# Attention output normalised by VectorE's 32x32 transposes, one power in the mixer's double layer norm, grouped tail tiles

## Chip, cores and metric

One core of one Trainium2 chip. The metric is the device time of one execution in microseconds (us), as the median of several executions. The profile of a kernel is one execution; its span is 1 to 2 us shorter than the device time of the same run.

Engines in the profile: PE is TensorE, PEld its weight loads, DVE is VectorE, ACT is ScalarE, POOL is GpSimd, SP is SyncE. In lines of the profile, `L1178` is a line of the kernel, `out<-in` are the program's names, `xN` is a count.

## The reference

Two identical layers, each of attention and a mixer, over `x` of 1 x 2048 x 448, 16 heads of 28:

```python
def _layernorm(x, eps=1e-5):
    m = jnp.mean(x, axis=-1, keepdims=True); v = jnp.var(x, axis=-1, keepdims=True)
    return (x - m) / jnp.sqrt(v + eps)

def _A_ref(x, wqkv, wo):                       # attention
    q, k, v = split_heads(x @ wqkv)            # ... cut
    p = softmax(einsum("bhqd,bhkd->bhqk", q, k) * 28 ** -0.5)
    return merge_heads(einsum("bhqk,bhkd->bhqd", p, v)) @ wo

def _B_ref(x, w1, w2, w3, w4):                 # mixer
    h  = gelu(_layernorm(x) @ w1)              # then four channel groups shifted by -1, +1, -2, +2 rows
    x1 = x + shifted(h) @ w2                   # ... cut
    return x1 + gelu(_layernorm(x1) @ w3) @ w4

x = x + _A_ref(_layernorm(x), ...); x = x + _B_ref(_layernorm(x), ...)    # twice
```

The mixer is called on `_layernorm(x)` and normalises that input again: a layer norm of a layer norm.

## The kernel before

A scheduler in Python plans all instructions of all engines from a list of tasks, by a plan of latest starts. `MOVES`, a list of (time, seed) pairs found by a search, perturbs the plan. The instruction order on each engine is fixed when the kernel is built, so the order is part of the kernel. When TensorE would idle in the plan, the scheduler puts filler matmuls on `ones_bf` there. They compute nothing; they keep its clock up (shown for the setup: between 12 and 14 us it was 0.50 before and 1.00 in e1, which adds 22 of them; 1.00 after and 0.50 in e2, which takes 17 away).

The normalisation of the attention output, 36 times per execution. `u_sb` holds heads x 32 rows on the partitions; row 28 of each 32 is the softmax sum. TensorE moves the sums across partitions, VectorE takes reciprocals and splits them into two bf16 parts, and TensorE spreads them back:

```python
def t_norm(si):                                          # before; waits and buffer handling cut
    if first: dve: u_sb = copy(ps[UBK])                  # 128 x W out of the PV bank
    else:     dve: u_sb = uin * fct + ps[UBK]
    # ... if not last: spill u_sb to DRAM, return
    dve: ub = cast_bf16(u_sb)
    for q4 in range(nq): pe: ps[b][:, 4*q4:4*q4+4] = ub[:, 128*q4:128*q4+128].T @ e28b      # sums
    dve: rs = reciprocal(ps[b]);  dve: rh[0:m] = bf16(rs);  dve: rh[16:16+m] = rs - rh[0:m]
    pe:  ps[b][0:32, 0:128] = rh.T @ ident
    dve: rT = copy(ps[b])
    for q4 in range(nq): pe: ps[b][:, 128*q4:...] = selq[:, 128*q4:...].T @ rT              # spread
    dve: otn[:, g, 0:W] = u_sb * ps[b]
```

The mixer's double layer norm has two powers in a chain, on GpSimd, with small VectorE steps between:

```python
def t_mixA(L, tiles, direct):                            # before; cut
    dve:  VAR = var + EPS
    pool: R1  = VAR ** -0.5
    dve:  T1 = R1 * R1;  dve: T1 = T1 * var;  dve: T1 = T1 + EPS
    pool: R12 = T1 ** -0.5
    dve:  R12 = R12 * R1
    for t in tiles: dve: xn = (x_res[t] - mean) * R12
    transposes(xn, xt)                                   # a DMA transpose
```

ScalarE evaluates the softmax exponentials out of PSUM, 2 or 3 banks of 512 columns at a time. Scores are written ahead into five banks, so TensorE and ScalarE overlap as long as the scores come in time (they are busy for 96% and 95% of the span).

## Time and profile before

Median of 4 runs 1104.1 us (1103.57 to 1109.55); span of the profiled run 1103.0 us.

| stretch of ScalarE's timeline | us |
|---|---|
| start to the first exponential | 31.7 |
| first to the end of the last exponential | 1026.6, of it 14.8 waiting |
| end of the last exponential to the end | 44.7 |

The page of the kernel before: busy time and share by engine, then TensorE's clock in 40 slices (tenths of full speed), the chain of work that ended last, and the costliest groups.

```profile
PE 1054.4 (96%) x9277; PEld 416.9 (38%) x9277; DVE 616.1 (56%) x1546; ACT 1049.8 (95%) x960; POOL 57.1 (5%) x82
...
PEclk7999999999999999999999999999999999999999
...
ACT 71%; PE 23%; DVE 4%; DMA 1%; issue 0%; SPq 0%; POOL 0%; ACTq 0%; DVEq 0%
...
L1178 ACT ACTIVATE PT<-ps 128x1536 bf16<-128x1536 f32 (+1 forms) x821 | 937.3, 1257 | 14.3 <-PE ps L1152 7.9
...
L1532 PE MATMUL ps<-ones_bf 128*128 128x256 bf16 x1153 | 173.0, 277 | 3.1 <-DVE ones_f L677 1.1
```

ScalarE is the bound: the chain is 71% ScalarE, and 937 of 1103 us are exponentials. TensorE's 96% contains 173 us of fillers. The only slice with a low clock is the first; a second half clock, of 3.4 us at 384 us, is too short to show in a slice.

The setup in windows of the kernel before: the window, its length, busy time of each engine with instruction counts, then the granted clock, DMA share and GB/s.

```profile
8.00:10.00 2.00, 0.82 (x10) 0.64 (x7) 0.00 (x0) 1.01 (x3) 2.00 (x4) 1.00 0.44 95
10.00:12.00 2.00, 0.38 (x6) 0.33 (x7) 0.93 (x2) 2.00 (x4) 1.79 (x3) 0.94 1.19 307
12.00:14.00 2.00, 1.75 (x13) 0.85 (x11) 1.33 (x8) 2.00 (x5) 0.60 (x1) 0.50 1.55 392
...
22.00:24.00 2.00, 2.00 (x6) 0.69 (x5) 1.50 (x5) 0.54 (x1) 0.87 (x1) 0.50 0.00 0
24.00:26.00 2.00, 2.00 (x8) 0.80 (x7) 1.03 (x3) 0.95 (x3) 0.00 (x0) 0.65 0.00 0
```

TensorE idles for 2.8 us (8.8 to 11.6), and its clock is halved from 11.8 until about 25.4 us, though from 12 to 26 us it is busy for 84% to 100% of each window of 2 us but one (20 to 22 us: 63%).

The tail in the chain of waits of the kernel before: start, us, what. It runs from the last normalisation to the first matmul on the transposed tile.

```profile
1065.55 0.15 DVE mst L1323
...
1067.57 0.54 POOL mst L1328
...
1068.13 0.17 DVE mst L1329
...
1068.33 0.53 DVE xn L1331
...
1068.89 2.30 DMA xT<-xn
```

### The profile page before, as it was taken

How to read it: one execution, taken by the hardware profiler on the slowest of the kernel's cores; microseconds unless marked ns; L12 is line 12 of the kernel's file. 1: busy time of each engine (PE TensorE's matmuls, PEld its weight loads, DVE VectorE, ACT ScalarE, POOL GpSimd, SP SyncE). 2: the span in 40 equal slices, each digit the busy share in tenths (PEclk: the TensorE clock that was granted, in tenths of full speed). 3: DMA queues.
4: the chain of work that ended last, by engine and by line, in shares of the span. 5: the costliest groups of instructions: out<-in, count | busy, mean ns of one | idle time of the engine just before them, and what ended most of it. 6: DMA issues, size and time to landing. Idle time of an engine off the chain costs nothing.

```text
span 1103.0 us, 21497 instructions
## 1 busy us (share of the span) xinstructions
PE 1054.4 (96%) x9277; PEld 416.9 (38%) x9277; DVE 616.1 (56%) x1546; ACT 1049.8 (95%) x960; POOL 57.1 (5%) x82
## 2 busy tenths in 40 slices
PE   8999999999999999999999999999999999999998
PEld 4333333343333333333333433343333333444465
DVE  5975247422654356743787354525886446486464
ACT  6999999999999999999799999999999999999954
POOL 3100000000000000000001000000010000010000
PEclk7999999999999999999999999999999999999999
DMA  7222071000000010000121101221201011100001
GB/s 194 58 86 59 20 190 21 15 2 20 1 20 20 1 39 11 10 20 1 40 39 44 27 32 49 77 67 50 57 1 34 10 25 11 37 21 11 11 28 36
DMA packets 79687, 41.27 MB, mean 37 GB/s; under 512 B 63912, under 2 KB 73000, under 8 KB 79592
## 3 DMA queue, kind: packets, MB, share of 16 engines
q1 hardware_dynamic: 77480, 36.23, 13.4%
q0 software_dynamic: 2112, 3.67, 1.3%
q8 instruction: 72, 1.18, 0.5%
q14 instruction: 23, 0.19, 0.1%
HBM read 14.20 MB, written 8.13 MB: 20 GB/s over the span
## 4 chain that ended last, share of the span: by engine, by line
ACT 71%; PE 23%; DVE 4%; DMA 1%; issue 0%; SPq 0%; POOL 0%; ACTq 0%; DVEq 0%
ACT PT L1178 64%; PE ps L645 11%; PE ps L1152 5%; ACT h2T L1478 4%; PE ps L1202 4%; PE ps L648 2%; ACT gt L1299 1%; PE ps L1532 1%; ACT L1478 1%; DMA xT<-xn 1%; ACT L1178 1%; DMA h2T<-in_A_wqkv_dram 1%; DVE qT L941 1%; DVE st L809 0%; DVE xn L875 0%
## 5 line engine op out<-in xcount | busy, mean ns | idle before, releaser
L1178 ACT ACTIVATE PT<-ps 128x1536 bf16<-128x1536 f32 (+1 forms) x821 | 937.3, 1257 | 14.3 <-PE ps L1152 7.9
L1152 PE MATMUL ps<-qT,kT 32*128 32x512 bf16 (+1 forms) x2304 | 320.1, 360 | 19.1 <-ACT PT L1178 13.1
L1202 PE MATMUL ps<-PT,vaug 128*32 128x512 bf16 (+1 forms) x2304 | 240.5, 362 | 1.7 <-ACT PT L1178 0.9
L1152 PEld LDWEIGHTS ps<-qT,kT 32*128 32x128 bf16 x2304 | 80.6, 91 | 264.2 <-ACT PT L1178 158.8
L1532 PE MATMUL ps<-ones_bf 128*128 128x256 bf16 x1153 | 173.0, 277 | 3.1 <-DVE ones_f L677 1.1
L645 PE MATMUL ps<-xT,w 112*128 112x512 bf16 (+5 forms) x684 | 129.6, 313 | 2.2 <-DMA xT<-xn 1.3
L1471 DVE CAST h2T<-ps 128x512 bf16<-128x512 f32 (+2 forms) x126 | 73.9, 586 | 97.8 <-PE ps L645 72.1
L1532 PEld LDWEIGHTS ps<-ones_bf 128*128 128x128 bf16 x1153 | 95.0, 98 | 76.5 <-issue 53.0
L1202 PEld LDWEIGHTS ps<-PT,vaug 128*32 128x32 bf16 x2304 | 61.4, 94 | 115.8 <-issue 66.4
L645 PE MATMUL ps<-w,h2T 128*128 128x448 bf16 x356 | 82.7, 360 | 5.7 <-ACT h2T L1478 5.0
L645 PEld LDWEIGHTS ps<-xT,w 112*128 112x128 bf16 (+1 forms) x684 | 52.1, 104 | 51.7 <-issue 25.7
L1486 DVE TENSOR_TENSOR x_res<-x_res,ps 128x448 f32<-128x448 f32 x32 | 19.6, 620 | 84.5 <-PE ps L645 70.0
L1478 ACT ACTIVATE h2T<-h2T 128x7168 bf16<-128x7168 bf16 (+2 forms) x9 | 45.1, 5016 | 7.3 <-DVE h2T L1471 7.2
L1221 DVE SCALAR_TENSOR_TENSOR u_sb<-uin,fct,ps 128x512 f32<-128x512 f32 x24 | 17.9, 746 | 58.2 <-PE ps L1202 53.7
L648 PE MATMUL ps<-xT,w 112*32 112x512 bf16 (+3 forms) x592 | 47.5, 335 | 0.5 <-DMA xT<-xn 0.3
L645 PEld LDWEIGHTS ps<-w,h2T 128*128 128x128 bf16 x356 | 30.2, 99 | 41.1 <-issue 13.4
L1217 DVE COPY u_sb<-ps 128x512 f32<-128x512 f32 (+1 forms) x36 | 22.7, 630 | 40.0 <-PE ps L1202 39.9
L809 DVE BATCH_NORM_STATS2 st<-x_res 128x6 f32<-128x448 f32 x60 | 36.5, 612 | 0.6
L1427 POOL TENSOR_TENSOR mst<-mst,neghalf 128x1 f32<-128x1 f32 x32 | 21.2, 669 | 293.2 <-DVE mst L1425 292.2
L1324 POOL TENSOR_TENSOR mst<-mst,neghalf 128x4 f32<-128x4 f32 (+2 forms) x10 | 9.1, 907 | 508.8 <-DVE mst L1323 508.8
L645 PE MATMUL ps<-xT,wk_pad 112*128 112x512 bf16 x106 | 32.3, 410 | 0.6 <-DVE kT L906 0.4
L906 DVE TENSOR_SCALAR qT<-ps,bcol 128x512 bf16<-128x512 f32 (+1 forms) x24 | 15.6, 659 | 29.6 <-PE ps L645 27.1
(149 smaller groups left out, 955.9 us busy)
## 6 DMA issues: line engine op xcount, KB each, us to landing
uscr<-u_sb SPq DMA_DIRECT2D x24, 256.0 KB, 2.0
uin<-uscr SPq DMA_DIRECT2D x24, 256.0 KB, 2.8
x_res<-in_A_x_dram POOLq DMA_DIRECT2D x4, 896.0 KB, 7.2
w<-in_B_w_dram SPq DMA_DIRECT2D x2, 1568.0 KB, 12.8
out_dram<-uin SPq DMA_DIRECT2D x16, 112.0 KB, 1.7
h2T<-in_A_wqkv_dram SPq DMA_DIRECT2D x2, 392.0 KB, 6.3
w<-in_B_w_dram SPq DMA_DIRECT2D x2, 392.0 KB, 7.5
xT<-xn SPq DMA_TRANSPOSE x37, 3.7
```

Of the source, the lines that this page charges most:

```text
L645: return e.matmul(out=dst(0, m), lhsT=lhs(0, m), rhs=rhs, start=start, stop=stop)
L648: return [e.matmul(out=dst(a, min(m, a + 32)), lhsT=lhs(a, min(m, a + 32)), rhs=rhs, start=start, stop=stop, tile_position=(0, a)) for a i ...
L809: yield op("dve", 0.55, lambda e: e.bn_stats(out=st6[:, t, :], in_=w4[:, t, :] if staged else x_res[:, t, :]), reads=[(("w4",), t // 2) if ...
L1152: yield op("pe", 0.005 if ph == h else 0.012 + W / 2400.0, lambda e, bk=bk, r0=32 * j, g=g, kc=kc, q0=q0, W=W, c0=W * h: e.matmul(out=ps[: ...
L1178: yield op("act", e_dur(n), lambda e, b0=b0, p0=p0, cnt=cnt: e.activation(out=PT[:, p0:p0 + cnt, :], in_=ps[:, b0:b0 + cnt, :], func=ACT.E ...
L1202: yield op("pe", 0.004 + nt * 0.0133, lambda e, j=j, rhs=rhs, vs=vs, i=i: e.matmul(out=ps[32 * j:32 * j + 32, UBK, 0:128 * nt], lhsT=vaug[ ...
L1217: yield op("dve", c_ps(W), lambda e: e.tensor_copy(out=u_sb[:, 0:W], in_=ps[:, UBK, 0:W]), reads=[("ps", UBK)], writes=[("u",)], last=[("p ...
L1427: yield op("pool", 1.0, lambda e, t=t: e.tensor_tensor(out=mst[:, t, R3:R3 + 1], in0=mst[:, t, V3E:V3E + 1], in1=neghalf[:, 0:1], op=ALU.pow),
L1471: yield op("dve", c_ps(NW), lambda e, fch=fch, b=b: e.tensor_copy(out=h2T[:, fch, hoff:hoff + NW], in_=ps[:, bi(b), 0:NW]), reads=[("ps", ...
L1478: yield op("act", c_act(14 * NW), lambda e: e.activation(out=h2T[:, :, hoff:hoff + NW], in_=h2T[:, :, hoff:hoff + NW], func=ACT.Gelu_apprx ...
L1486: yield op("dve", c_ps(D), lambda e, t=t, b=b: e.tensor_tensor(out=x_res[:, t, :], in0=x_res[:, t, :], in1=ps[:, bi(b), 0:D], op=ALU.add), ...
L1532: SC.fill = (0.13, lambda e, b: e.matmul(out=ps[:, bi(b), 0:256], lhsT=ones_bf[:, :], rhs=ones_bf[:, :].unsqueeze(1).to_broadcast([128, 2, ...
```

## The change

The intent: normalise without PSUM and TensorE. A VectorE transpose turns each 32 x 32 block of `u_sb` so that the softmax sums lie along the free axis, beside the values they divide. A reciprocal and one product with a broadcast follow, and a second transpose turns back. The two powers become one, because 1/sqrt(v+e) times 1/sqrt(v/(v+e)+e) equals (v(1+e)+e^2)^-1/2. In the tail, the DMA transposes become TensorE transposes, the last two tiles share their matmuls, and the final cast is folded into the residual addition. The setup is rearranged as well, and the order was searched anew (new `MOVES`).

```diff
-    dve: u_sb = copy(ps[UBK])
+    if last: dve: u_sb = transpose32(ps[UBK])           # else the copy stays
-    dve: ub = cast(u_sb);  pe: sums;  dve: reciprocal, rh, rh;  pe: rh.T;  dve: rT;  pe: spread;  dve: otn = u_sb * ps
+    if not first: dve: gt = transpose32(u_sb)           # tb is gt, or u_sb where it is transposed already
+    dve: rs = reciprocal(tb[:, :, DH])
+    dve: tn = tb[:, :, 0:DH] * rs                       # 32-column blocks, rs broadcast
+    dve: otn[:, g, 0:W] = transpose32(tn)
@@ mixer
-    VAR, R1 = VAR**-0.5, T1 (three steps), R12 = T1**-0.5, R12 * R1
+    dve: T1 = var * (1 + EPS) + EPS*EPS;  pool: R12 = T1 ** -0.5
+    # R1, which only the residual needs, in a task of its own
@@ tail
-    transposes(xs, xt, n)                # by DMA
+    transposes(xs, xt, n, direct)        # direct: four TensorE transposes and one copy per tile
+TAILB = [[NT - 3], [NT - 2, NT - 1]]     # the second MLP of the last two tiles in one piece
-    x_res += ps;  out = cast(x_res)
+    out = bf16(x_res + ps)
@@ setup (cut): one initialisation in place of two on ScalarE, pad casts that may go to VectorE, other DMA order
@@ MOVES (cut): all seeds new
```

## The prediction

> **What bounds it now.** ScalarE. The page has it 95% busy; the 821 softmax exponentials alone take 937 us, and exponentials are 64% of the chain of waits. TensorE's 96% is misleading: 173 us of it are filler matmuls (1153 of them) that only keep it busy. VectorE is 56% busy. In time (ScalarE's timeline):
> - setup, 31.7 us until the first exponential;
> - the steady part, 31.7 to 1058.3 us, where ScalarE waits only about 14 us. 5.5 of that is at the layer boundary (524 to 533 us) and 2.9 near 1040 to 1050; both times a lump of second-MLP matmuls (`w,h2T`) stands between the scores;
> - the tail, 44.7 us, bound by TensorE and by a chain of small VectorE steps.
>
> **Normalisation (36 times).** Removed: 292 small matmuls (30 us busy by the groups), the casts and reciprocal-splitting on VectorE (about 31 us) and the PSUM product (22.5). Added: two transposes, a product, and for 12 spilled segments a third transpose. [...] no transpose is in this trace. [...] So VectorE changes little in sum, and TensorE's saving becomes filler: off the critical path in the steady part. It counts once, in the tail: from the last PV to `otn` is 3.7 us now, about 1.7 after.
>
> **Mixer's layer norm.** One power instead of two chained ones (0.55 to 0.9 us each) and three fewer VectorE steps. Off the path until the tail, where about 1.7 us falls away (1065.5 to 1068.3 now).
>
> **Tail.** The 2.3 us DMA transpose becomes four TensorE transposes and a copy, about 1.2. Grouping the last two tiles makes 56 matmuls of 256 columns from 112 of 128: 0.067 us each at 128, about 0.117 at 256, so about 1 us of TensorE, and ScalarE's 42 small gelus become 28. The final cast (0.4 us) is folded into the addition. From about 1071 to 1100 us TensorE stays nearly full, 28 us of work before and about 29 after, so only the chain ahead of it and the end shorten: about 5 us.
>
> **Setup.** ScalarE loses 1.9 us of initialisation and two casts (to VectorE), and one `xn` is done early. The K projection should start 1.5 to 3 us before its present 15.95. Today TensorE idles from 8.8 to 11.6 us and its clock is halved from 11.9 to 25.8 us; if the new order avoids that, more is won. The first scores move ahead of eight V and eight Q matmuls, but that work then delays the second segment. Estimate: 3.5 us.
>
> **Steady part.** Exponentials, tanh, nine gelu table switches: unchanged. The instruction order was searched anew: at the layer boundary the gelu now comes about 30 exponentials before the break instead of 5, so the lump is spread. I expect the 14 us of waiting to fall to 7 or 8.
>
> **Sum.** 1103.8 − 3.5 − 6.5 − 5.5 = **1088 us, 80% range 1081 to 1095**. Chances: faster by over 2% 0.14, within 2% 0.855, slower 0.005.
>
> **Right if:** the first exponential starts near 27 to 29 us; ScalarE shows no wait over 2 us at the boundary; from the last exponential to the end 38 to 41 us; the exponential group stays at 937 us; filler matmuls rise by some 70.
>
> **Wrong if:** the VectorE transpose from PSUM is far slower than a copy, holding the PV bank and delaying scores; the new order stalls where the old did not; setup keeps the halved clock and the second segment stalls; or, upward, the clock stays full in setup.

The 1.7 us from the last PV to `otn` was the author's estimate; the trace of before leads near it with two transposes as long as its PSUM copy of 128x256 (0.42 us each), a reciprocal (0.20) and a product (0.42), 1.5 us without the hand-overs. The 0.067 us for a matmul of 128 columns is read from the trace of before (88 in 5.93 us), the 0.117 for 256 columns is an estimate (46 fillers of 256 columns took 5.18 us there, 0.113 each).

## The result, and the profile after

After: median of 4 runs 1091.13 us (1090.71 to 1091.6). Ratio 0.987, 95% interval 0.9844 to 0.9897: within 2%. A ratio here is the measuring program's own, from runs of both kernels in the same rounds; it is not quite the ratio of the medians.

Both profiled spans, divided where the prediction divided them:

| stretch | before | after | difference | predicted |
|---|---|---|---|---|
| start to first exponential | 31.72 | 22.82 | -8.90 | -3.5 |
| first to end of last exponential | 1026.61 | 1028.11 | +1.50 | -6.5 |
| end of last exponential to end | 44.67 | 38.37 | -6.30 | -5.5 |
| span | 1103.0 | 1089.3 | -13.7 | -15.5 |

The page of the kernel after, the same lines:

```profile
PE 1048.6 (96%) x9482; PEld 411.8 (38%) x9501; DVE 610.5 (56%) x1414; ACT 1044.3 (96%) x938; POOL 59.5 (5%) x80
...
PEclk9999999999999999999999999999999999999999
...
ACT 57%; PE 36%; DVE 5%; issue 1%; DMA 0%; SPq 0%; ACTq 0%; DVEq 0%
...
L1181 ACT ACTIVATE PT<-ps 128x1536 bf16<-128x1536 f32 (+1 forms) x821 | 938.8, 1247 | 12.6 <-PE ps L1155 10.1
...
L1540 PE MATMUL ps<-ones_bf 128*128 128x256 bf16 x1225 | 180.8, 276 | 2.6 <-DVE hot L673 1.1
```

The exponentials are nearly as before. The chain goes through TensorE for a larger part (36% in place of 23%), though ScalarE is as busy as it was. Fillers rise by 72. The low clock of the first slice is gone. The setup in windows of the kernel after:

```profile
8.00:10.00 2.00, 1.27 (x18) 0.96 (x16) 1.53 (x7) 2.00 (x5) 2.00 (x4) 1.00 0.36 87
10.00:12.00 2.00, 1.54 (x20) 1.14 (x18) 0.98 (x2) 2.00 (x4) 1.49 (x3) 1.00 1.43 379
12.00:14.00 2.00, 1.55 (x15) 0.90 (x13) 1.26 (x7) 1.78 (x2) 0.00 (x0) 1.00 1.55 388
```

But the early start does not all count. ScalarE's timeline of the first exponentials (start, length, group, idle before it), first of the kernel before, then of the kernel after:

```profile
31.72 7.32 ACT L1178 ACTIVATE PT<-ps 128x1536 bf16<-128x1536 f32 x6
39.28 6.09 ACT L1178 ACTIVATE PT<-ps 128x1536 bf16<-128x1536 f32 x5 [0.24 <-PE ps L1152]
```

```profile
22.82 7.14 ACT L1181 ACTIVATE PT<-ps 128x1536 bf16<-128x1536 f32 x6 [0.20 <-PE ps L1155]
34.90 2.37 ACT L1181 ACTIVATE PT<-ps 128x1536 bf16<-128x1536 f32 x2 [4.93 <-PE ps L1155]
```

The seventh exponential takes the first scores of the second segment (the second group of four heads), whose query projection comes late on TensorE. It starts at 34.90 in place of 39.28. So of 8.9 us, 4.4 are left. Counted from the seventh exponential to the end of the last, before has 1019.05 us (14.36 of it idle), after 1016.03 (8.72 idle): -3.0. Most of ScalarE's idle time lies in its waits for scores (`qT,kT` matmuls) and PV matmuls; the view of waits, from the first exponential on, lists them by the line waited for, before and then after (us in total, times, longest):

```profile
ACT PT L1178 <- PE ps L1152: 7.9, 12, 3.3
ACT PT L1178 <- PE ps L1202: 5.0, 5, 2.2
```

```profile
ACT PT L1181 <- PE ps L1155: 10.1, 14, 4.9
```

The waits of 5.5 us at the layer boundary are gone (0.32 and 0.72 are left there), and so are the 2.9 near 1040 to 1050. The wait of 4.9 is the new one in the setup.

The new normalisation in the steady part, VectorE's timeline of the kernel after:

```profile
336.65 0.72 DVE L1221 STREAM_TRANSPOSE u_sb<-ps 128x512 f32<-128x512 f32 x1
337.40 0.25 DVE L1244 RECIPROCAL rs<-u_sb 128x16 f32<-128x16 f32 x1
337.69 0.62 DVE L1245 TENSOR_TENSOR tn<-u_sb,rs 128x448 bf16<-128x448 f32 x1
338.35 0.71 DVE L1254 STREAM_TRANSPOSE otn<-tn 128x512 bf16<-128x512 bf16 x1
338.99 0.65 DVE L1471 CAST h2T<-ps 128x512 bf16<-128x512 f32 x1
```

A transpose of 128x512 takes 0.72 us from PSUM and 0.71 us in bf16 out of SBUF, as long as a PSUM copy of that size (0.69); out of SBUF in f32 it takes 0.71 us too. For 128x256 it is 0.45 us from PSUM and 0.44 in bf16 out of SBUF. In the tail, the corresponding chain:

```profile
1056.04 0.15 DVE L1331 TENSOR_SCALAR mst<-mv 128x1 f32<-128x1 f32 x1
...
1056.92 0.48 DVE L1335 TENSOR_SCALAR xn<-x_res,mv,mst 128x448 bf16<-128x448 f32 x1
...
1057.93 0.42 DVE L855 COPY xT<-ps 112x512 bf16<-112x512 bf16 x1 [0.40 <-PE ps L850]
```

From the first small step to the normalised tile: 0.88 us in place of 2.78. From the tile to its transpose: about 1.0 in place of 2.3.

### The profile page after: what moved, and what is told of

Read it like the earlier page. It is cut to its first block, busy times and chain, and to the rows that moved or that the text cites. A ratio compares the mean times of both kernels' runs of the same rounds, so it can differ in the third digit from the quotient of the medians.

```text
span 1089.3 us, 21738 instructions
## 1 busy us (share of the span) xinstructions
PE 1048.6 (96%) x9482; PEld 411.8 (38%) x9501; DVE 610.5 (56%) x1414; ACT 1044.3 (96%) x938; POOL 59.5 (5%) x80
## 4 chain that ended last, share of the span: by engine, by line
ACT 57%; PE 36%; DVE 5%; issue 1%; DMA 0%; SPq 0%; ACTq 0%; DVEq 0%
ACT PT L1181 50%; PE ps L639 10%; PE ps L1155 10%; PE ps L1205 8%; PE ps L642 4%; PE ps L1540 4%; ACT h2T L1478 4%; ACT gt L1297 1%; ACT L1478 1%; ACT L1181 1%; DMA h2T<-in_A_wqkv_dram 0%; DVE qT L909 0%; ACT h2T L1468 0%; DVE hT L1288 0%; DVE qT L944 0%
## 5 line engine op out<-in xcount | busy, mean ns | idle before, releaser
L1181 ACT ACTIVATE PT<-ps 128x1536 bf16<-128x1536 f32 (+1 forms) x821 | 938.8, 1247 | 12.6 <-PE ps L1155 10.1
L1205 PE MATMUL ps<-PT,vaug 128*32 128x512 bf16 (+1 forms) x2304 | 263.6, 362 | 3.0 <-ACT PT L1181 0.8
L1540 PE MATMUL ps<-ones_bf 128*128 128x256 bf16 x1225 | 180.8, 276 | 2.6 <-DVE hot L673 1.1
L1540 PEld LDWEIGHTS ps<-ones_bf 128*128 128x128 bf16 x1225 | 102.1, 98 | 81.2 <-issue 57.9
L639 PE MATMUL ps<-xT,w 112*128 112x512 bf16 (+6 forms) x581 | 118.1, 324 | 1.6 <-DVE h2T L1471 0.6
L639 PE MATMUL ps<-w,h2T 128*128 128x448 bf16 x302 | 68.9, 354 | 5.3 <-ACT h2T L1478 5.0
L639 PEld LDWEIGHTS ps<-xT,w 112*128 112x128 bf16 (+1 forms) x581 | 45.7, 104 | 49.3 <-issue 26.0
L642 PE MATMUL ps<-xT,w 112*32 112x512 bf16 (+3 forms) x780 | 63.6, 340 | 0.3 <-DVE uin L1489 0.2
L642 PE MATMUL ps<-w,h2T 128*32 128x448 bf16 x584 | 46.4, 368 | 4.5 <-ACT h2T L1478 4.5
L1496 DVE TENSOR_TENSOR x_res<-x_res,ps 128x448 f32<-128x448 f32 x16 | 9.8, 619 | 71.2 <-PE ps L639 48.5
L642 PEld LDWEIGHTS ps<-xT,w 112*32 112x32 bf16 (+1 forms) x780 | 24.0, 95 | 11.8 <-DVE hT L1288 0.6
```

The costliest lines, as they stand in the source:

```text
L639: return e.matmul(out=dst(0, m), lhsT=lhs(0, m), rhs=rhs, start=start, stop=stop)
L642: return [e.matmul(out=dst(a, min(m, a + 32)), lhsT=lhs(a, min(m, a + 32)), rhs=rhs, start=start, stop=stop, tile_position=(0, a)) for a i ...
L1181: yield op("act", e_dur(n), lambda e, b0=b0, p0=p0, cnt=cnt: e.activation(out=PT[:, p0:p0 + cnt, :], in_=ps[:, b0:b0 + cnt, :], func=ACT.E ...
L1205: yield op("pe", 0.004 + nt * 0.0133, lambda e, j=j, rhs=rhs, vs=vs, i=i: e.matmul(out=ps[32 * j:32 * j + 32, UBK, 0:128 * nt], lhsT=vaug[ ...
L1540: SC.fill = (0.13, lambda e, b: e.matmul(out=ps[:, bi(b), 0:256], lhsT=ones_bf[:, :], rhs=ones_bf[:, :].unsqueeze(1).to_broadcast([128, 2, ...
```

## The experiments

Theories at the start. **A**: the sum of the prediction, with the clock as the reason for the large gain in the setup; VectorE is off the path in the steady part. **B**: the clock is a bystander, and the setup gained by its rearrangement alone. **C**: the operations bring the gain. **D**: the new search of the order brings it. There were twelve runs, in three lots on different chips; each lot ran the kernel before beside it (medians 1103.39, 1104.81 and 1103.82 us). The kernel after was not among these rounds, so small differences from it are read in the traces.

### Runs 1 and 2: the hole in the setup

`e1_before_setup_filler` fills TensorE's hole in the kernel before; `e2_after_setup_hole` opens one in the kernel after.

```diff
 # e1, on the planned order of the kernel before
+new = [filler matmul into bank 3] * 22
+pe[54:54] = new                     # straight after the first four transposes
 # e2, on the planned order of the kernel after
+remove the 17 filler matmuls between the first transposes and the K projection
```

> The kernel before, order unchanged, with 22 filler matmuls put into the hole of TensorE between 8.8 and 11.6 us of the setup. Theory A (the setup is paced by TensorE, and its halved clock from 11.9 to 25.8 us is what made it slow): the granted clock stays at 1.0 through the setup, the first exponential moves from 31.7 to 27 to 29 us, the K projection's first four matmuls take about 1.0 us in place of 1.9, and the whole kernel is 3 to 4.5 us faster than before, because nothing stalls behind it there. Theory B (the setup is paced by the loads and the ScalarE and VectorE chain, the clock is a bystander): under 1.5 us faster.

> The changed kernel, order unchanged, without the 17 filler matmuls that stand between its first transposes and the K projection. Theory A: the granted clock falls to 0.5 for some 10 us of the setup, the first exponential moves from 22.8 to 26 to 28 us, and the whole is 2 to 4 us slower than the changed kernel (about 1093 to 1095 us); less than the shift of the first exponential, since the wait of 4.9 us before the second segment takes up a part. Theory B: the first exponential moves by less than 1.5 us. A third outcome, in which the clock does not fall without the fillers, would say that the earlier projections alone keep it up.

The windows of e1, and then of e2:

```profile
10.00:12.00 2.00, 2.00 (x23) 1.81 (x22) 1.43 (x4) 2.00 (x4) 1.78 (x3) 1.00 1.13 287
12.00:14.00 2.00, 1.58 (x18) 0.96 (x16) 1.02 (x5) 2.00 (x4) 0.60 (x1) 1.00 1.55 398
```

```profile
10.00:12.00 2.00, 0.66 (x8) 0.47 (x8) 1.43 (x4) 2.00 (x5) 1.49 (x3) 0.81 1.33 349
12.00:14.00 2.00, 1.04 (x10) 0.80 (x11) 1.09 (x5) 2.00 (x2) 0.00 (x0) 0.50 1.56 391
...
18.00:20.00 2.00, 1.24 (x21) 0.85 (x20) 1.67 (x6) 0.36 (x1) 0.00 (x0) 0.98 1.35 326
```

ScalarE's first exponentials in e1:

```profile
27.44 7.29 ACT L1178 ACTIVATE PT<-ps 128x1536 bf16<-128x1536 f32 x6
34.97 10.82 ACT L1178 ACTIVATE PT<-ps 128x1536 bf16<-128x1536 f32 x9 [0.24 <-PE ps L1152]
```

In e1 the clock stays at 1.00 throughout the setup. The first exponential starts at 27.44 (31.72 without fillers), the seventh at 34.97 (39.28). That is 4.3 us, from instructions that compute nothing. Of it, 2.9 are left in the span (1100.1): the tail of that run is 1.0 us longer, and 0.4 went between. In time, e1 is 1102.11 us (1100.64 to 1109.91), ratio 0.9995, interval 0.9966 to 1.0024: the rounds don't show the 2.9 us, and the 3 to 4.5 us expected for the whole kernel were missed. The kernel before itself spreads by 6 us in these rounds. The spread goes with the granted clock: its seven runs at 0.994 or 0.995 took 1101.9 to 1103.5 us, its four at 0.989 to 0.991 took 1105.5 to 1108.0. The four runs of e1 at 0.997 or 0.998 average 1.6 us less than those seven, a choice made after the fact.

In e2 the clock falls to 0.50 at about 11.2 us and returns at about 18.1. First exponential 24.91 (+2.1), seventh 36.98 (+2.1), span 1090.5 (+1.2); time 1092.94 us, ratio to before 0.9897. The effect is about half of that in e1, and the low clock lasted 7 us in place of 14. It is also less than expected (10 us of low clock, first exponential at 26 to 28, 2 to 4 us in all). The stall before the seventh exponential stays (4.94 us).

What follows: B falls as the whole story. In the kernel before, the clock alone cost 4.3 us at the seventh exponential; the rearranged setup with a full clock gained 4.4 there. At full clock the two setups are even at that point (34.97 in e1, 34.90 in the kernel after): the earlier first scores were paid back in the stall. But the two don't add up to neat shares, as e2 shows: with a low clock for half as long as in the kernel before, the new setup keeps 2.3 of its 4.4 us.

### Runs 3 and 4: the operations without the search

```diff
-est, P, SC = attempt(plan, MOVES)
+est, P, SC = attempt(plan, ())
```

> The kernel before with its list of perturbations of the order empty: the same operations in the scheduler's plain order. Theory C (the operations of the change bring most of the gain, the new search only keeps pace with them): slower than before by 25 to 45 us, nearly all of it as waits of ScalarE between the exponentials; the distance to the changed kernel treated in the same way is 10 to 20 us. Theory D (the new search of the order is the gain, the operations bring little): that distance is under 5 us.

> The changed kernel with its list of perturbations empty. Theory C: faster than the unsearched kernel before by 10 to 20 us, with the difference in the setup and the tail and only a few us of it in the steady part. Theory D: within 5 us of the unsearched kernel before.

Before without its searched order: 1135.88 us (1131.06 to 1137.61), ratio 1.0279. After without: 1113.35 us (1112.48 to 1117.13), ratio 1.0089 to the searched kernel before. The distance is 22.5 us, more than the 13 between the searched kernels. ScalarE's waits for scores fell from 40.5 to 18.4 us, by the groups of e3 and then of e4:

```profile
L1178 ACT ACTIVATE PT<-ps 128x1536 bf16<-128x1536 f32 (+1 forms) x821 | 938.8, 1251 | 44.2 <-PE ps L1152 40.5 <-PE ps L1202 2.0
```

```profile
L1181 ACT ACTIVATE PT<-ps 128x1536 bf16<-128x1536 f32 (+1 forms) x821 | 939.3, 1247 | 26.5 <-PE ps L1155 18.4 <-PE ps L1205 6.3
```

By the medians, the search is worth 31.8 us to the kernel before (1135.88 to 1104.1) and 22.2 to the kernel after (1113.35 to 1091.13). So D, with its distance under 5 us, falls: in the plain order the changed kernel, its rearranged setup included, is 22 us ahead. Theory C is not borne out as it was written either. It put the distance at 10 to 20 us, mostly in the setup and the tail. Of the 25.1 us between the two profiled spans, 3.3 lie before the first exponential, 4.4 in the tail and 17.5 between the first and the last exponential. e3 has 41 us of half clock in five episodes, e4 10 in two. Which operation brings the 17.5 us, or whether the plain plan of e3 merely stalls more by chance, no run shows: a scheduler answers the edit here as in runs 5 to 8 below. A reading of the smaller distance with the search, argued and not shown: the old search had already hidden much of what the change removes, so less was left to gain in the steady part. A stall of 5.06 us in the setup is in e4 too, so it didn't come with the search.

### Runs 5 to 8: the tail, one part undone at a time, with a new plan

These keep the order up to the last scores, and let the scheduler plan the tail anew for each variant. `e9_after_tail_replanned` is the control without an edit.

```diff
 # e6: for part in TAILB  ->  for part in [[t] for t in tb]       (no grouping)
 # e7: if on_pe           ->  if False                            (DMA transposes)
 # e8: the two chained powers of the kernel before, in the tail only
```

> Control for the three tail experiments. The changed kernel with no operation changed; only the instructions from about the last score matmuls on are ordered by the scheduler's plain plan and not by the searched order. Every theory expects the changed kernel's time within 1.5 us: 1090 to 1092.5 us.

> The control with the last two 128-row tiles of the tail not grouped: 112 matmuls of 128 columns in place of 56 of 256, 42 small gelus in place of 28. Theory A (grouping saves TensorE about 1 us, and the gelus are off the path): 0.5 to 2 us longer than the control. Rival (grouping delays the first of the two tiles' layer norm and so costs what it saves): equal or shorter.

> The control with the transposes of the normalised mixer input in the tail given back to the DMA, as in the kernel before. Theory A (the chain from layer norm to the transposed tile sets the tail's start; 2.3 us by DMA against 0.9 us by TensorE and a copy): 1 to 2.5 us longer than the control. Rival (TensorE's work bounds the tail and the chain hides under it): within 0.5 us.

> The control with the two chained powers of the double layer norm, and their small VectorE steps, put back in the tail alone. Theory A (the chain is on the path there): 1.3 to 2.5 us longer than the control. Rival (only a part of the chain is on the path): under 1 us longer.

| kernel | median us (lowest to highest) | ratio to before | tail in the trace, us |
|---|---|---|---|
| e9, control | 1094.76 (1093.84 to 1095.15) | 0.9899 | 41.7 |
| e6, single tiles | 1093.49 (1092.70 to 1094.24) | 0.9889 | 41.1 |
| e7, DMA transposes | 1093.90 (1092.43 to 1095.08) | 0.9893 | 40.8 |
| e8, two powers | 1097.02 (1094.72 to 1097.75) | 0.9917 | 44.2 |

The control missed its expectation: its tail is 41.7 us against 38.4 of the searched order. Two "worse" variants beat it. So the plain plan costs 3 us in the tail whatever the operations are, and it differs from variant to variant by as much as the operations themselves. e6 and e7 prove nothing about the grouping or the transposes. e8 fits theory A in size (+2.3), but its trace also has a clock of 0.68 between 1075 and 1080 us, which the control has not. This design was weak: to let a scheduler answer an edit is to change two things.

### Runs 9 to 11: edits with the order frozen

These edit the finished instruction lists of the kernel after and leave all other instructions in place.

```diff
 # e10, tail only: T1 and pow of the last two tiles repeated twice, in a chain
+T1, pow -> T1, pow, T1, pow, T1, pow -> xn
 # e11, tail only: the first two times four TensorE transposes and a copy -> one DMA transpose
 # e5, everywhere: each of the 144 VectorE steps of the normalisation run twice in a row
+transpose, transpose, reciprocal, reciprocal, product, product, transpose, transpose
```

> The changed kernel with the power of the double layer norm, and the small VectorE step ahead of it, run three times in a chain instead of once, for the last two tiles of the tail only; the order of all other instructions is untouched, so this needs no control. The chain to the normalised tile grows by about 1.7 us (two more of 0.15 us on VectorE plus 0.6 us on GpSimd and hand-overs). Theory A (this chain sets when the tail's matmuls start): 1.3 to 2.5 us longer. Rival (only part of it is on the path): under 1 us longer.

> The changed kernel with the first two TensorE transposes of the tail (four matmuls and a copy each) given back to the DMA, one tile each, the order of all other instructions untouched. The DMA took 2.3 us from issue to landing in the trace of before, the four matmuls and the copy take 0.9 us. Theory A (on the path): 1.0 to 2.5 us longer. Rival (TensorE's work bounds the tail and the transposes hide under it, as the experiment with the replanned order suggests): within 0.5 us.

> The changed kernel with every one of the 144 VectorE steps of the normalisation (transposes, reciprocal, product) run twice in a row, order otherwise unchanged. VectorE gains about 75 us of work (estimate: 24 x 0.69 + 12 x 0.71 + 36 x (0.2 + 0.65 + 0.7) us, from the durations in the trace of the changed kernel). Theory A (VectorE is off the path except in the last unit): last exponential less than 3 us later, tail about 1.5 us longer, whole kernel 1.5 to 4.5 us longer. Rival (VectorE's 56% hides a path through it, so that its durations reach ScalarE): 10 us or more longer.

The tail in the traces, us from the end of the last exponential:

| | before | after | e10 | e11 |
|---|---|---|---|---|
| first normalised tile (`xn`) starts | 10.0 | 6.0 | 7.9 | 6.0 |
| first matmul on its transpose | 12.9 | 7.5 | 9.4 | 8.9 |
| end | 44.7 | 38.4 | 41.6 | 39.6 |

The two normalised tiles in e10, each after a wait for the added power:

```profile
1058.14 0.51 DVE L1340 TENSOR_SCALAR xn<-x_res,mv,mst 128x448 bf16<-128x448 f32 x1 [0.66 <-POOL mst L1337]
...
1061.21 0.51 DVE L1340 TENSOR_SCALAR xn<-x_res,mv,mst 128x448 bf16<-128x448 f32 x1 [0.66 <-POOL mst L1337]
```

In e10 the chain grew by 1.9 us at the first tile, and the end came 3.2 us later. The second tile paid twice, since its chain stands behind the first on VectorE. Its `xn` starts at 11.0 us in place of 7.3. Time 1095.38 us, ratio 0.9916; the span is 2.5 us longer than that of the kernel after, since its last exponential happened to end 0.7 us earlier. In e11 the matmuls start 1.4 us later and the tail is 1.2 us longer. The timeline of e11 shows TensorE waiting for it:

```profile
1060.07 1.10 PE L639 MATMUL ps<-xT,w 112*112 112x128 bf16 x16 [2.45 <-DMA xT<-xn]
```

Time 1093.01 us, ratio 0.9896. Theory A holds for both: the chain from the layer norm to the transposed tile sets the tail's end. The rivals fall. The clock stayed at 1.00 in both tails. e10's tail overshot the 2.5 us of theory A by 0.7.

e5 is the miss: 1156.02 us (1151.49 to 1162.11), ratio 1.0467. VectorE's busy time rose by 76 us as planned (610.5 to 686.8), and the tail by 1.6, as expected. But the last exponential ended 60.3 us later. ScalarE waits 61.8 us before exponentials in place of 12.6. One stretch of e5 shows how; first VectorE's timeline, then TensorE's, then the windows:

```profile
353.35 1.47 DVE L1225 STREAM_TRANSPOSE u_sb<-ps 128x512 f32<-128x512 f32 x2
354.86 0.54 DVE L1248 RECIPROCAL rs<-u_sb 128x16 f32<-128x16 f32 x2
355.43 1.28 DVE L1249 TENSOR_TENSOR tn<-u_sb,rs 128x448 bf16<-128x448 f32 x2
356.75 1.46 DVE L1258 STREAM_TRANSPOSE otn<-tn 128x512 bf16<-128x512 bf16 x2
358.13 1.38 DVE L1475 CAST h2T<-ps 128x512 bf16<-128x512 f32 x2
```

```profile
358.84 0.62 PE L642 MATMUL ps<-xT,w 112*32 112x512 bf16 x8 [1.86 <-DVE h2T L1475]
```

```profile
355.00:360.00 5.00, 3.14 (x34) 0.89 (x34) 4.30 (x8) 2.77 (x3) 0.00 (x0) 0.94 0.02 3
360.00:365.00 5.00, 5.00 (x31) 0.99 (x31) 0.69 (x1) 3.57 (x3) 0.00 (x0) 0.50 0.00 0
365.00:370.00 5.00, 5.00 (x21) 1.01 (x23) 1.38 (x2) 3.14 (x4) 0.00 (x0) 0.50 0.00 0
370.00:375.00 5.00, 5.00 (x35) 1.11 (x27) 0.69 (x1) 3.75 (x4) 0.00 (x0) 0.70 0.01 2
```

The four steps of the normalisation stand in a row on VectorE: 2.4 us once, 4.8 us doubled. The cast that frees a PSUM bank for the mixer's matmuls stands behind them, and TensorE stops for 1.86 us. Half a microsecond after it goes on, its clock is halved, for 13.7 us. TensorE is full now, its scores come late, and ScalarE waits 6.7 us before the exponentials between 360 and 375 us. VectorE idles meanwhile. In e5 there are eight such episodes, 61 us of half clock in all. The kernel after has one, of 3.4 us. But the episodes are not the whole of it: of the 61.8 us of waits, about 32 lie from 4 us before such an episode to 6 us after it. The rest is spread over the run; 4.9 of it is the stall in the setup.

So "VectorE is off the path" is true of its busy share and false of its bursts. The theory as I wrote it falls. What is shown is the mechanism in this stretch; what isn't shown is what causes the waits away from the episodes, and how much of the 60 us would remain if the order were searched for these durations. e5 keeps an order that was tuned to the shorter ones.

The holes can be counted. In the traces of before, after and e5, TensorE has 25 holes of 1.5 to 2.8 us after the setup's first 6 us. After 11 of them the granted clock fell to half; after 14 it didn't. The hole of 2.21 us that ends at 1013.5 us in the kernel after was followed by half clock there and in e8, e9 and e11. The same hole at nearly the same place in e2, e6, e7 and e10 was not. The episodes differ in length. The windows show 3.4 us (before from 383.8 us, after from 1014.3), 6.8 (setup of e2), 10.2 (setup of e3) and 13.7 us (setup of before, and e5 from 359.4).

The length of a hole does not decide alone. One of 1.97 us (before, ending at 382.70 us) was followed by half clock from 383.80 us. One of 2.03 us (after, ending at 494.04) was not, nor was the one of 2.45 us in e11's tail (ending at 1060.07, the clock 1.00 there). What decides is not shown.

### Run 12: an attempt to mend the setup, failed

The stall before the seventh exponential invited a mend. On TensorE, the third head group's query projection goes ahead of the second's, and VectorE spends 2.4 us on the next chunk's `xn` before the steps that the second group waits for. `e12_after_setup_reordered` changed that order by hand.

```diff
+pe:  Q(group 2) ahead of Q(group 3); scores of group 2 ahead of the next chunk's K projection
+dve: cast, square, bias of group 2 ahead of group 3's
+every wait worked out again from the recorded dependences
```

> The changed kernel with the order in the setup mended by hand: the query projection of the second head group goes ahead of the third group's, its VectorE steps follow at once, and its scores stand ahead of the key projection of the next chunk; no operation is added or taken away. Theory A (ScalarE's 4.93 us stall at 30 us is an accident of the order on TensorE and VectorE): the stall falls to 1.5 to 3 us and the kernel to 1088 to 1089.5 us. Rival (the VectorE work before the stall is needed anyway, and what is put off stalls ScalarE later): the stall moves and the time stays within 0.7 us.

The result was right and took 2054.53 us (1977.81 to 2094.79). That is no answer to the question but a mistake of mine: the recorded dependences include those between two TensorE matmuls that follow each other on the same bank, which the kernel leaves out of its waits (e2, e10 and e11, which leave them out too, gave right results). With them, matmuls waited for matmuls: a filler's mean rose from 276 to 364 ns, a score matmul's from 360 to 480, and the granted clock fell to 0.66. Whether the stall can be mended stays open. No version of mine beats the kernel after.

## Why the prediction was right or wrong

Right in the total: 1088 predicted, 1091.13 measured, inside the range of 1081 to 1095, and within 2%. That the total is so close is luck in part: two of its three terms were mis-sized, by -5.4 and +8.0 us, and these errors nearly cancel. Of its own tests, "first exponential near 27 to 29" failed, and two of the cases under "wrong if" came about: the clock stayed full in the setup, and the new order stalled where the old did not (4.93 us before the second segment).

- **Setup, -3.5 us: mis-sized, -8.9 measured.** The first exponential was to start "near 27 to 29 us"; it started at 22.82. The prediction had named the reason ("if the new order avoids that, more is won") and didn't price it. e1 prices it: 4.3 us. It had also said that the work put off "then delays the second segment": 4.93 us, shown. Net at the seventh exponential -4.4.
- **Steady part, -6.5 us: mis-sized, +1.5 measured.** It is +1.5 by the prediction's own division, since the stall falls into it; from the seventh exponential on it was -3.0. The waiting there fell from 14.4 to 8.7 us, near the "7 or 8" foretold. But ScalarE's busy time rose by 2.6 us, of which 1.5 are in the exponentials (937.3 to 938.8). Single exponentials did not get longer (their mean fell from 1257 to 1247 ns), so neighbours overlap less. No run isolates that, and its cause stays open. Waits at the layer boundary: none over 2 us, right.
- **Tail, -5.5 us: right in mechanism, -6.3 measured.** Last PV to `otn`, counted from VectorE's first step on it: 3.7 to 1.6 us (predicted 1.7). Power chain: 2.78 to 0.88 (predicted -1.7, measured -1.9); e10 shows that it is on the path, and costs more than its length when put back. Transposes: 2.3 to about 1.0; e11 shows 1.2 us of the tail. The tail was to be 38 to 41 us; it is 38.4. TensorE's stretch was 28.5 and is 28.9, its new transposes included. What the grouping alone brings stays open, because e6 could not separate it.
- **Normalisation off the path in the steady part: not tested by itself in this kernel, wrong as a rule.** No run puts the old normalisation back, so that its saving brings nothing there is argued. Removed: TensorE's 292 small matmuls; fillers rose by 72 ("some 70"). VectorE's sum changed little (616.1 to 610.5). The transpose took 0.71 us, near the 0.69 of the PSUM copy. But e5 shows little slack: another 2.4 us in a burst reaches ScalarE through TensorE's clock. The prediction read slack from a share of 56%.
- **Order searched anew: a gain does not need it.** Without the searches the distance is 22.5 us (e3, e4), more than with them, though a plain plan has luck of its own.

## What to carry to other kernels

Where TensorE's clock depends on its being busy, a short hole can cost more than its length (2.8 us cost 4.3 us in this setup; 14 of the 25 holes counted were not followed by a lower clock): look for the holes, then at the clock in windows behind them, and do not count fillers as waste. Slack of an engine whose order the kernel fixes is the slack of the instruction behind a burst and not its idle share (here VectorE, 56% busy: another 2.4 us in one burst of e5 was followed by a stop of TensorE for 1.86 us and by 13.7 us of half clock); double the burst to find out. To test one part of a change in a scheduled kernel, edit the finished lists and keep all else in place, and check that the edit brings no waits that the original leaves out.
